# Attention and expert kernel on one core: the two heads' scores as 64-row products on the halves of the array

## The chip, the cores and the metric

The kernel runs on one core of one Trainium2 chip. The metric is the device time in microseconds (us) of that core from launch to end; lower is better. The engines are named as in the profile: PE (TensorE matmuls), PEld (its weight loads), DVE (VectorE), ACT (ScalarE), POOL (GpSimd), SP (SyncE, which issues all DMAs here). Matmuls write to banks of PSUM; the kernel's tiles of 128 x 512 fp32 take one bank each, and it uses eight.

## The reference

Attention over 8 batches, 8 heads, 576 positions, head size 64, then one feed-forward block over the 4608 tokens. Heads 0 to 3 see a local window, heads 4 to 7 a strided set:

```python
scores = scale * np.matmul(q, k.transpose(0, 1, 3, 2))
rel = pos[:, None] - pos[None, :]
mask_local = (rel >= 0) & (rel < 32)
mask_strided = (rel >= 0) & (pos[None, :] % 32 == pos[:, None] % 32)
scores = np.where(masks, scores, -1e9)          # local for h < 4, else strided
attn = exp(scores - max) / (sum + 1e-9)
x = (attn @ v), heads side by side              # 4608 x 512
h = x @ w_in                                    # 512 -> 2048
out = (h * erf(softplus(h))) @ w_out            # 2048 -> 512
```

## The kernel before, in words

Attention is cut into 96 pieces: 8 batches, four pairs of heads (`hp`; 0 and 1 local, 2 and 3 strided), three parts `j` of the sequence. A piece has up to two blocks of `n` queries against 128 keys: `n` is 96 for a local piece; for a strided one, where positions are regrouped by their residue modulo 32, it is 126 with two blocks for `j` 0 and 1, and 72 with one block for `j` 2. The two heads of a pair lie on partitions 0 to 63 and 64 to 127.

`scores` (L261) makes one fp32 product per block over all 128 partitions: the stationary operand is the keys of both heads, the moving operand has the queries of head 0 with zeros on partitions 64 to 127, beside the queries of head 1 with zeros on 0 to 63. So both heads' scores come out side by side in one bank `s`. Then, in this order, `mask` (DVE, L282, adds the mask while it copies to `sm`), `maxi` (POOL, L287, the maximum over partitions), `sub` (DVE, L296), `exp` (ACT, L300), `av` (PE, L304, into bank `pav`), `total`, `invert` and `norm` (DVE, L315 to L329), `transp` (PE, L335, into bank `pt`), `split_hi` (ACT, L353) and `split_lo_x` (DVE, L358), which write the tokens to a ring as a high and a low half (`xhi`, `xlo`).

Batches 0 and 1 differ: with `pe_mask` the mask is added on PE by a bf16 product with the identity (L271), and ACT copies the result (L279). In batch 0 (`early`) the maximum is subtracted on PE too (L291), inside the bank, which `exp` then reads; there `s` comes from the tag `h` (three banks) and `pav` from an `o` bank. In all other batches `s` and `pav` share the tag `ps` (two banks) with `pt`, which takes it in every batch.

The feed-forward block works in 12 chunks of 384 tokens, each in 16 tiles of 128 hidden units. A tile has 12 products `mm1` (L457, three terms of a high and low split) into a bank of tag `h`, a chain of ACT (L465, L495) and DVE (L462, L492, L498) steps, and 9 products `mm2` (L527) into three banks `o`. The weights arrive as 64-bit words and are unpacked by DVE (L408, L415, L421, L429) and ACT (L426). In the first part of the run PE fills idle time with products that nobody reads (`warm`, L638).

The order on every engine is written out by a planner (`Plan.order`). Each step has an engine, an estimated duration, a due time (`key`), predecessors, tiles that it takes and tiles that it uses. The planner goes through simulated time and always emits, for each engine, the ready step with the earliest due time; a step that takes a tile is ready only once the users of the tile that held that buffer before are done. Due times of pieces and expert tiles come from constants at the top (`PRO`, `SLOT`, `A0K` and others). At run time semaphores enforce the same dependencies in the emitted order.

Of the kernel before, what the change touches and what calls it, by code (L numbers as in the profile page):

```python
# [18 lines left out]
P = 128  # L19
# [21 lines left out]
RB = 7  # L41
NA = S // 32
QS = RB * NA
WL = 2 * 2 * QL + 2 * QL + 32
WS = 2 * 2 * QS + 2 * P
WV = 2 * 2 * (D + 1)
NCON = 2 * QL + QS + P
NEG = -1.0e30
# [40 lines left out]
class Plan:  # L89
# [18 lines left out]
    def _ready(self, op, live):  # L108
        t = op.earliest
        for p in op.after:  # L110
            if p.end is None:
                return None
            t = max(t, p.end + (self.SAME if p.eng == op.eng else self.LATENCY)[op.eng])
        for b in op.new:
            order = live.setdefault(b.tag, [])
            n = len(order) - self.bufs[b.tag]
            if n >= 0:
                for u in order[n].users:
                    if u.end is None:
                        return None  # L120
                    t = max(t, u.end + (self.SAME if u.eng == op.eng else self.LATENCY)[op.eng])
        return t
# [46 lines left out]
def attention_moe(  # L169
# [37 lines left out]
    def buf(pool, tag, shape, name, dtype=F32):  # L207
        def make():
            return pools[pool].tile(shape, dtype, tag=tag, name=name, bufs=bufs[tag])

        return Buf(tag, make)
# [8 lines left out]
    def piece(b, hp, j, key, dt, ring, pe_mask=False, pool_sub=False, early=False):  # L220
# [8 lines left out]
        pid = f"{b}_{hp}_{j}"  # L229
        qk = buf("apool", "qk", [P, WS], f"qk_{pid}")  # L230
        v = buf("apool", "v", [P, 2, 2, D + 1], f"v_{pid}")
        s = buf("ps_h", "h", [P, 512], f"s_{pid}") if early else buf("ps_a", "ps", [P, 512], f"s_{pid}")
        sm = buf("apool", "sm", [P, 4 * QS], f"sm_{pid}")
        mx = buf("apool", "mx", [P, 4 * QS], f"mx_{pid}")
        pav = buf("ps_o", f"o{hp % 2}", [P, 512], f"av_{pid}") if early else buf("ps_a", "ps", [P, 512], f"av_{pid}")
# [4 lines left out]
        def load_qk():  # L240
            if loc:
                yield nc.sync.dma_start(qk[:, :WL], qk_loc[b, hp, j])
            else:
                w = nblk * (2 * n + P)
                yield nc.sync.dma_start(qk[:, :w], qk_str[b, hp - 2, j, :, :w])

        def load_v():
            w = nblk * 2 * (D + 1)
            yield nc.sync.dma_start(v.tile.rearrange("p b h d -> p (b h d)")[:, :w], v_all[b, hp, j, :, :w])

        def masks():
            if loc:
                m = mask_l if j == 0 else mask_l[:, 1:2]
                return m.broadcast_to([P, 2, 2, n]), "p (b h q) -> p b h q", dict(b=2, h=2)
            return mask_s[:, :, :n].broadcast_to([P, units, n]), "p (u q) -> p u q", dict(u=units)

        def scores():
            k0, step = units * n, n if loc else P
            for blk in range(nblk):
                dst = s[:, blk * 2 * n : (blk + 1) * 2 * n]  # L260
                yield nc.tensor.matmul(  # L261
                    dst,
                    qk[:, k0 + blk * step : k0 + blk * step + P],
                    qk[:, blk * 2 * n : (blk + 1) * 2 * n],
                    start=blk == 0,
                    stop=not pe_mask,
                    skip_group_check=True,
                )
                if pe_mask:
                    m = (mask_l[:, int(j > 0 or blk > 0)] if loc else mask_s[:, :, :n]).broadcast_to([P, 2, n])  # L270
                    yield nc.tensor.matmul(  # L271
                        dst.rearrange("p (h q) -> p h q", h=2), ident_b, m, start=False, stop=True,
                        skip_group_check=True,
                    )

        def mask():
            src, dst = s[:, :cols], sm[:, :cols]
            if pe_mask:
                yield nc.scalar.copy(dst, src)  # L279
            else:  # L280
                m, r, sizes = masks()
                yield nc.vector.tensor_tensor(  # L282
                    out=dst.rearrange(r, **sizes), in0=src.rearrange(r, **sizes), in1=m, op=ALU.add
                )

        def maxi():
            yield nc.gpsimd.partition_all_reduce(mx[:, :cols], sm[:, :cols], P, ReduceOp.max)  # L287

        def sub():
            if early:  # L290
                yield nc.tensor.matmul(  # L291
                    s[:, :cols], neg, mx[:, :cols], start=False, stop=True, skip_group_check=True
                )
            else:
                d = sm[:, :cols]
                yield (nc.gpsimd if pool_sub else nc.vector).tensor_tensor(out=d, in0=d, in1=mx[:, :cols], op=ALU.subtract)  # L296

        def exp():
            d = sm[:, :cols]
            yield nc.scalar.activation(d, s[:, :cols] if early else d, AF.Exp, scale=1.0 / D**0.5)  # L300

        def av():
            for u in range(units):
                yield nc.tensor.matmul(  # L304
                    pav[:n, u * (D + 1) : (u + 1) * (D + 1)],
                    sm[:, u * n : (u + 1) * n],
                    v[:, u // 2, u % 2, :],
                    start=True,
                    stop=True,
                )  # L310
# [48 lines left out]

        add = plan.add  # L360
        w = nblk * n
        lq = add("sp", P * 4 * (WL if loc else nblk * (2 * n + P)) / 3.6e5, key - 8.0, load_qk, new=[qk])
        lv = add("sp", P * 4 * nblk * 2 * (D + 1) / 3.6e5, key - 7.9, load_v, new=[v])
        per = max(2 * n / 600.0, 0.213) + (2 * n / 2400.0 if pe_mask else 0.0)
        o_s = add("pe", 0.02 + nblk * per, key, scores, [lq, *o_con], [s, sm], [qk])
        if pe_mask:
            o_m = add("act", act(cols, 0.06), key + 0.1, mask, [o_s], [], [s, sm])
        else:
            o_m = add("dve", dve(cols), key + 0.1, mask, [o_s], [], [s, sm])
        o_x = add("pool", 0.4 + cols * 0.0028, key + 0.2, maxi, [o_m], [mx], [sm], earliest=6.7)  # L370
        if early:
            o_b = add("pe", cols / 600.0, key + dt, sub, [o_x], [], [mx, s])
        elif pool_sub:
            o_b = add("pool", 0.1 + cols / 450.0, key + 0.3, sub, [o_x], [], [mx, sm])
        else:
            o_b = add("dve", dve(cols), key + dt, sub, [o_x], [], [mx, sm])
        o_e = add("act", act(cols), key + dt + 0.1, exp, [o_b], [], [sm, s] if early else [sm])
        o_v = add("pe", 0.00174*n * units, key + dt + 0.2, av, [o_e, lv], [pav, xn], [sm, v])
        o_r = add("dve", 0.07, key + 1.5 * dt, total, [o_v], [rc], [pav])
        o_r = add("dve", 0.1, key + 1.5 * dt, invert, [o_r], [], [rc])  # L380
# [269 lines left out]
def _layout(q, k, v):  # L650
    import numpy as np

    f32 = np.float32
    hl = H // 2

    def pairs_t(a):

        a = a.reshape(B, 2, 2, S, D).transpose(0, 1, 2, 4, 3)
        return np.ascontiguousarray(a).reshape(B, 2, 2 * D, S)

    def resid(a):
        return np.ascontiguousarray(a.reshape(B, hl, NA, 32, D).transpose(0, 1, 3, 2, 4)).reshape(B, hl, S, D)

    qk_loc = np.zeros((B, 2, 3, P, WL), f32)
    qk_str = np.zeros((B, 2, 3, P, WS), f32)
    v_all = np.zeros((B, 4, 3, P, 2, 2, D + 1), f32)
    v_all[..., D] = 1.0

    ql, kl = pairs_t(q[:, :hl]), pairs_t(k[:, :hl])
    kl = np.concatenate([np.zeros((B, 2, 2 * D, 32), f32), kl], axis=3)  # L670
    vl = v[:, :hl].reshape(B, 2, 2, S, D)
    vl = np.concatenate([np.zeros((B, 2, 2, 32, D), f32), vl], axis=3)
    qb = qk_loc[..., : 4 * QL].reshape(B, 2, 3, P, 2, 2, QL)
    for j in range(3):
        for blk in range(2):
            i = 2 * j + blk
            for h in range(2):
                qb[:, :, j, h * D : (h + 1) * D, blk, h] = ql[:, :, h * D : (h + 1) * D, i * QL : (i + 1) * QL]
                v_all[:, :2, j, :, blk, h, :D] = vl[:, :, h, i * QL : i * QL + P]
        qk_loc[:, :, j, :, 4 * QL :] = kl[..., j * 2 * QL : j * 2 * QL + 2 * QL + 32]  # L680
    qk_loc[..., : 4 * QL] = qb.reshape(B, 2, 3, P, 4 * QL)

    qs, ks, vs = resid(q[:, hl:]), resid(k[:, hl:]), resid(v[:, hl:])
    qs, ks = pairs_t(qs), pairs_t(ks)
    vs = vs.reshape(B, 2, 2, S, D)
    for j in range(3):
        nblk = 2 if j < 2 else 1
        n = QS if j < 2 else S - 4 * QS
        for blk in range(nblk):
            p0 = (2 * j + blk) * QS  # L690
            for h in range(2):
                hs, c0 = slice(h * D, (h + 1) * D), (2 * blk + h) * n
                qk_str[:, :, j, hs, c0 : c0 + n] = qs[:, :, hs, p0 : p0 + n]
            k0 = nblk * 2 * n + blk * P
            qk_str[:, :, j, :, k0 : k0 + n] = ks[..., p0 : p0 + n]
            for h in range(2):
                v_all[:, 2:, j, :n, blk, h, :D] = vs[:, :, h, p0 : p0 + n]
    return qk_loc, qk_str, v_all.reshape(B, 4, 3, P, WV)
# [45 lines left out]
```

## Time and profile before

| | us |
|---|---|
| median of 3 runs | 994.0 |
| lowest and highest | 993.76, 994.02 |
| the profiled execution, own time | 993.13 |
| its span (first to last instruction) | 991.2 |
| PE busy | 979.5 |
| DVE busy | 728.7 |
| ACT busy | 654.7 |
| POOL busy | 152.8 |

How to read the rows: a row of grouped instructions has line, engine, operation, written tile <- read tiles, shape and count, then busy us and mean ns of one, then the engine's idle time just before them with what ended it. In a row of the timeline or of the chain the first two numbers are the start and the length in us, and `x4` says that four neighbours were merged. Matmuls are pipelined, so the lengths of neighbours overlap; the time that a group really takes on PE is read from start to start.

### The profile page before, as it was taken

To read this page: it belongs to the slowest core of one execution; us is meant where nothing else is said; L and a number is where in the kernel's file an instruction comes from. 1 tells how busy PE (TensorE), PEld (TensorE's weight loads), DVE (VectorE), ACT (ScalarE), POOL (GpSimd) and SP (SyncE) were. 2 spreads that over 40 slices of the span, in tenths; PEclk is the share of its full clock that TensorE was granted. 3 is DMA by queue.
4 is the path that set the end of the run, shared out by engine and by line. 5 is a ranking of instruction groups with operands and counts; after the bars stand their busy time and mean duration, and the time that the engine had idled before them with its cause. 6 is when DMAs were issued, how large, how long until landed. Compare 5 with 4: busy or idle time off the path is not lost.

```text
span 991.2 us, 15250 instructions
## 1 busy us (share of the span) xinstructions
PE 979.5 (99%) x5443; PEld 885.6 (89%) x5443; DVE 728.7 (74%) x1619; ACT 654.7 (66%) x1481; POOL 152.8 (15%) x100
## 2 busy tenths in 40 slices
PE   8999999999999999999999999999999999999998
PEld 6788999999899989999899999999899999999997
DVE  6999997677677776676777776776767776665664
ACT  4676777567566666666765665766766576766765
POOL 3534111111112110011112110111111210000000
PEclk9999999999999999999999999999999999999999
DMA  9994211111222211111222220211112220000000
GB/s 310 308 338 144 63 35 59 40 40 53 71 62 82 62 37 38 46 53 27 80 58 73 71 63 19 70 40 40 49 53 66 63 63 1 32 2 0 32 1 33
DMA packets 37659, 68.76 MB, mean 69 GB/s; under 512 B 4176, under 2 KB 18640, under 8 KB 37584
## 3 DMA queue, kind: packets, MB, share of 16 engines
q1 hardware_dynamic: 37584, 67.80, 22.1%
q8 instruction: 43, 0.70, 0.3%
q14 instruction: 32, 0.26, 0.1%
HBM read 58.34 MB, written 9.44 MB: 68 GB/s over the span
## 4 chain that ended last, share of the span: by engine, by line
PE 91%; DVE 8%; ACT 0%; issue 0%; DMA 0%
PE h L457 39%; PE o L527 39%; PE s L261 5%; PE av L304 5%; DVE w L415 1%; PE t L335 1%; DVE w L421 1%; DVE pair L429 1%; DVE a L462 1%; DVE w L408 1%; DVE glo L498 1%; DVE b L492 0%; DVE xlo L358 0%; DVE b L462 0%; PE warm L638 0%
## 5 line engine op out<-in xcount | busy, mean ns | idle before, releaser
L527 PE MATMUL o<-pair,ghi 128*128 128x512 f32 x1152 | 372.3, 404 | 0.0
L457 PE MATMUL h<-xhi,pair 128*128 128x384 f32 x1536 | 306.7, 341 | 1.4 <-DVE b L492 1.4
L457 PEld LDWEIGHTS h<-xhi,pair 128*128 128x128 f32 x1536 | 271.9, 188 | 15.7 <-DVE b L492 3.8
L465 ACT ACTIVATE b<-b 128x384 f32<-128x384 f32 x384 | 199.7, 521 | 104.2 <-DVE b L462 101.6
L287 POOL PARTITION_ALL_REDUCE mx<-sm x96 | 152.6, 1594 | 664.1 <-DVE sm L282 568.7
L527 PEld LDWEIGHTS o<-pair,ghi 128*128 128x128 f32 x1152 | 207.0, 188 | 28.0
L527 PE MATMUL o<-pair,glo 128*128 128x512 f32 x576 | 225.9, 392 | 0.0
L457 PE MATMUL h<-xlo,pair 128*128 128x384 f32 x768 | 165.9, 337 | 0.0
L498 DVE TENSOR_TENSOR glo<-b,ghi 128x384 fp32r<-128x384 f32 x192 | 110.5, 576 | 60.3 <-ACT ghi L495 59.8
L462 DVE SCALAR_TENSOR_TENSOR a<-h,a 128x384 f32<-128x384 f32 x192 | 106.4, 554 | 64.9 <-ACT a L465 63.3
L457 PEld LDWEIGHTS h<-xlo,pair 128*128 128x128 f32 x768 | 137.2, 187 | 0.0
L462 DVE SCALAR_TENSOR_TENSOR a<-a,h 128x384 f32<-128x384 f32 x192 | 105.5, 549 | 40.7 <-ACT b L465 38.6
L465 ACT ACTIVATE b<-a 128x384 f32<-128x384 f32 x192 | 100.5, 524 | 47.6 <-DVE glo L498 47.1
L527 PEld LDWEIGHTS o<-pair,glo 128*128 128x128 f32 x576 | 108.1, 188 | 24.1
L495 ACT CAST ghi<-b 128x384 fp32r<-128x384 f32 x192 | 97.9, 510 | 46.8 <-PE o L527 41.6
L492 DVE TENSOR_TENSOR b<-b,h 128x384 f32<-128x384 f32 x192 | 105.1, 547 | 31.2 <-ACT b L465 30.9
L465 ACT ACTIVATE a<-a 128x384 f32<-128x384 f32 x192 | 100.2, 522 | 26.6 <-DVE a L462 24.3
L465 ACT ACTIVATE a<-h 128x384 f32<-128x384 f32 x192 | 92.7, 483 | 33.4 <-PE h L457 32.3
L462 DVE SCALAR_TENSOR_TENSOR b<-b,a 128x384 f32<-128x384 f32 x192 | 110.5, 576 | 3.2
L304 PEld LDWEIGHTS av<-v,sm 128*96 128x96 f32 (+2 forms) x704 | 78.0, 171 | 7.8 <-ACT sm L300 1.5
L261 PE MATMUL s<-qk 128*128 128x192 f32 (+2 forms) x352 | 83.4, 351 | 0.1
L304 PE MATMUL av<-v,sm 128*96 128x65 f32 (+2 forms) x704 | 77.9, 251 | 1.1 <-ACT sm L279 0.7
(34 smaller groups left out, 588.4 us busy)
## 6 DMA issues: line engine op xcount, KB each, us to landing
qk<-qk_loc SPq DMA_DIRECT2D x48, 304.0 KB, 2.8
qk<-qk_str SPq DMA_DIRECT2D x32, 380.0 KB, 3.2
v<-v_all SPq DMA_DIRECT2D x80, 130.0 KB, 2.1
out<-ob SPq DMA_DIRECT2D x36, 256.0 KB, 2.1
words<-w_in SPq DMA_DIRECT2D x16, 512.0 KB, 5.6
words<-w_out SPq DMA_DIRECT2D x16, 512.0 KB, 5.9
qk<-qk_str SPq DMA_DIRECT2D x16, 136.0 KB, 2.1
v<-v_all SPq DMA_DIRECT2D x16, 65.0 KB, 1.9
```

The source lines that it names most:

```text
L261: yield nc.tensor.matmul(dst, qk[:, k0 + blk * step : k0 + blk * step + P], qk[:, blk * 2 * n : (blk + 1) * 2 * n], start=blk == 0, stop=n ...
L287: yield nc.gpsimd.partition_all_reduce(mx[:, :cols], sm[:, :cols], P, ReduceOp.max)
L304: yield nc.tensor.matmul(pav[:n, u * (D + 1) : (u + 1) * (D + 1)], sm[:, u * n : (u + 1) * n], v[:, u // 2, u % 2, :], start=True, stop=True,)
L335: yield nc.tensor.transpose(pt[:, blk * n : (blk + 1) * n], xn[:n, 2 * blk : 2 * blk + 2, :].rearrange("p h d -> p (h d)"), ident[:n, :n],)
L408: yield nc.vector.tensor_scalar(out=w.tile.bitcast(U32), in0=words[:, :, 1], scalar1=0x07FFFFFF, scalar2=3, op0=ALU.bitwise_and, op1=ALU.l ...
L457: yield nc.tensor.matmul(ph[:, :CH], win[4 * s + cc][:, w, fs], x[cc][:, c0 : c0 + CH], start=(i == 0), stop=(i == len(terms) - 1))
L462: yield nc.vector.scalar_tensor_tensor(out=out, in0=in0, scalar=scalar, in1=in1, op0=op0, op1=op1)
L465: yield nc.scalar.activation(dst, src, func, bias=bias[i], scale=scale)
L492: yield nc.vector.tensor_tensor(out=bb.tile, in0=bb.tile, in1=ph[:, :CH], op=ALU.mult)
L495: yield nc.scalar.copy(ghi.tile, bb.tile)
L498: yield nc.vector.tensor_tensor(out=glo.tile, in0=bb.tile, in1=ghi.tile.bitcast(F32), op=ALU.subtract)
L527: yield nc.tensor.matmul(po.tile, g[:, ts], wout[f][:, w], start=(f == 0 and i == 0), stop=(f == NFC - 1 and i == 2),)
```

## The change

Each block's score product becomes two, one for each head, over 64 partitions (0 to 63 and 64 to 127). The queries lie without zeros in one block of columns for both heads. Each head writes a bank of its own, `s[0]` and `s[1]`, with all blocks of the head side by side; in batch 0 `s[0]` comes from the tag `h` and `s[1]` from `ps`, in the others both come from `ps`. The order of columns in `sm` changes from block-head to head-block, and `av` reads accordingly. The mask on DVE, the mask product on PE, the copy on ACT, and in batch 0 the subtracting product and the exponential, run once per head on half the columns. The loads of queries and keys get narrower. The planner counts two tiles of one tag in one step, and is given new durations.

```diff
-WL = 2 * 2 * QL + 2 * QL + 32
-WS = 2 * 2 * QS + 2 * P
+WL = 2 * QL + 2 * QL + 32
+WS = 2 * QS + 2 * P
...
-        for b in op.new:
+        for i, b in enumerate(op.new):
             order = live.setdefault(b.tag, [])
-            n = len(order) - self.bufs[b.tag]
+            n = len(order) - self.bufs[b.tag] + sum(x.tag == b.tag for x in op.new[:i])
...
-        s = buf("ps_h", "h", [P, 512], f"s_{pid}") if early else buf("ps_a", "ps", [P, 512], f"s_{pid}")
+        s = [
+            buf("ps_h", "h", [P, 512], f"s{h}_{pid}") if early and h == 0 else buf("ps_a", "ps", [P, 512], f"s{h}_{pid}")
+            for h in range(2)
+        ]
...
         def scores():
-            k0, step = units * n, n if loc else P
+            k0, step = half, n if loc else P
             for blk in range(nblk):
-                dst = s[:, blk * 2 * n : (blk + 1) * 2 * n]
-                yield nc.tensor.matmul(
-                    dst,
-                    qk[:, k0 + blk * step : k0 + blk * step + P],
-                    qk[:, blk * 2 * n : (blk + 1) * 2 * n],
-                    start=blk == 0,
-                    stop=not pe_mask,
-                    skip_group_check=True,
-                )
-                if pe_mask:
...
+                for h in range(2):
+                    rows = slice(h * D, (h + 1) * D)
                     yield nc.tensor.matmul(
+                        s[h][:, blk * n : (blk + 1) * n],
+                        qk[rows, k0 + blk * step : k0 + blk * step + P],
+                        qk[rows, blk * n : (blk + 1) * n],
+                        start=blk == 0,
+                        stop=not pe_mask,
                         skip_group_check=True,
                     )
+            if pe_mask:
+                for h in range(2):
+                    yield nc.tensor.matmul(
+                        s[h][:, :half].rearrange("p (b q) -> p b q", b=nblk), ident_b, masks(),
+                        start=False, stop=True, skip_group_check=True,
+                    )
 
         def mask():
-            src, dst = s[:, :cols], sm[:, :cols]
...
+            for h in range(2):
+                src, dst = s[h][:, :half], sm[:, h * half : (h + 1) * half]
...
         def exp():
...
+            if early:
+                for h in range(2):
+                    yield nc.scalar.activation(
+                        sm[:, h * half : (h + 1) * half], s[h][:, :half], AF.Exp, scale=1.0 / D**0.5
+                    )
...
-        per = max(2 * n / 600.0, 0.213) + (2 * n / 2400.0 if pe_mask else 0.0)
-        o_s = add("pe", 0.02 + nblk * per, key, scores, [lq, *o_con], [s, sm], [qk])
+        per = 0.235 + (2 * n / 2400.0 if pe_mask else 0.0)
+        o_s = add("pe", 0.08 + nblk * per, key, scores, [lq, *o_con], [*s, sm], [qk])
...
-            o_m = add("dve", dve(cols), key + 0.1, mask, [o_s], [], [s, sm])
+            o_m = add("dve", dve(cols) + 0.067, key + 0.1, mask, [o_s], [], [*s, sm])
```

More of the change, by code (lines that the diff above doesn't have):

```diff
@@ L243, in load_qk @@
             else:
-                w = nblk * (2 * n + P)
+                w = nblk * (n + P)
                 yield nc.sync.dma_start(qk[:, :w], qk_str[b, hp - 2, j, :, :w])
@@ L249, in load_v @@
             yield nc.sync.dma_start(v.tile.rearrange("p b h d -> p (b h d)")[:, :w], v_all[b, hp, j, :, :w])
+        half = nblk * n
         def masks():
@@ L253, in masks @@
                 m = mask_l if j == 0 else mask_l[:, 1:2]
-                return m.broadcast_to([P, 2, 2, n]), "p (b h q) -> p b h q", dict(b=2, h=2)
-            return mask_s[:, :, :n].broadcast_to([P, units, n]), "p (u q) -> p u q", dict(u=units)
+                m = m.rearrange("p b h q -> p b (h q)")
+                return m.broadcast_to([P, 2, n]) if j else m
+            return mask_s[:, :, :n].broadcast_to([P, nblk, n])
         def scores():
-            k0, step = units * n, n if loc else P
+            k0, step = half, n if loc else P
@@ L259, in scores @@
             for blk in range(nblk):
-                dst = s[:, blk * 2 * n : (blk + 1) * 2 * n]
-                yield nc.tensor.matmul(
-                    dst,
-                    qk[:, k0 + blk * step : k0 + blk * step + P],
-                    qk[:, blk * 2 * n : (blk + 1) * 2 * n],
-                    start=blk == 0,
-                    stop=not pe_mask,
-                    skip_group_check=True,
-                )
-                if pe_mask:
-                    m = (mask_l[:, int(j > 0 or blk > 0)] if loc else mask_s[:, :, :n]).broadcast_to([P, 2, n])
-                    yield nc.tensor.matmul(
-                        dst.rearrange("p (h q) -> p h q", h=2), ident_b, m, start=False, stop=True,
+                for h in range(2):
+                    rows = slice(h * D, (h + 1) * D)
+                    yield nc.tensor.matmul(
+                        s[h][:, blk * n : (blk + 1) * n],
[3 more added lines that the diff above has]
+                        stop=not pe_mask,
@@ L273, in scores @@
                         skip_group_check=True,
                     )
-        def mask():
-            src, dst = s[:, :cols], sm[:, :cols]
[L278 to L284, printed above, removed]
+            if pe_mask:
[4 more added lines that the diff above has]
+                    )
@@ L286, in maxi @@
+        def mask():
+            for h in range(2):
+                src, dst = s[h][:, :half], sm[:, h * half : (h + 1) * half]
+                if pe_mask:
+                    yield nc.scalar.copy(dst, src)
+                else:
+                    yield nc.vector.tensor_tensor(
+                        out=dst.rearrange("p (b q) -> p b q", b=nblk),
+                        in0=src.rearrange("p (b q) -> p b q", b=nblk), in1=masks(), op=ALU.add,
+                    )
         def maxi():
@@ L290, in sub @@
             if early:
-                yield nc.tensor.matmul(
-                    s[:, :cols], neg, mx[:, :cols], start=False, stop=True, skip_group_check=True
-                )
+                for h in range(2):
+                    yield nc.tensor.matmul(
+                        s[h][:, :half], neg, mx[:, h * half : (h + 1) * half], start=False, stop=True,
+                        skip_group_check=True,
+                    )
             else:
@@ L298, in exp @@
         def exp():
-            d = sm[:, :cols]
-            yield nc.scalar.activation(d, s[:, :cols] if early else d, AF.Exp, scale=1.0 / D**0.5)
+            if early:
+                for h in range(2):
+                    yield nc.scalar.activation(
+                        sm[:, h * half : (h + 1) * half], s[h][:, :half], AF.Exp, scale=1.0 / D**0.5
+                    )
+            else:
+                yield nc.scalar.activation(sm[:, :cols], sm[:, :cols], AF.Exp, scale=1.0 / D**0.5)
         def av():
@@ L305, in av @@
                     pav[:n, u * (D + 1) : (u + 1) * (D + 1)],
-                    sm[:, u * n : (u + 1) * n],
+                    sm[:, (u % 2) * half + u // 2 * n : (u % 2) * half + (u // 2 + 1) * n],
                     v[:, u // 2, u % 2, :],
@@ L361, in piece @@
         w = nblk * n
-        lq = add("sp", P * 4 * (WL if loc else nblk * (2 * n + P)) / 3.6e5, key - 8.0, load_qk, new=[qk])
+        lq = add("sp", P * 4 * (WL if loc else nblk * (n + P)) / 3.6e5, key - 8.0, load_qk, new=[qk])
         lv = add("sp", P * 4 * nblk * 2 * (D + 1) / 3.6e5, key - 7.9, load_v, new=[v])
-        per = max(2 * n / 600.0, 0.213) + (2 * n / 2400.0 if pe_mask else 0.0)
-        o_s = add("pe", 0.02 + nblk * per, key, scores, [lq, *o_con], [s, sm], [qk])
+        per = 0.235 + (2 * n / 2400.0 if pe_mask else 0.0)
+        o_s = add("pe", 0.08 + nblk * per, key, scores, [lq, *o_con], [*s, sm], [qk])
         if pe_mask:
-            o_m = add("act", act(cols, 0.06), key + 0.1, mask, [o_s], [], [s, sm])
+            o_m = add("act", act(cols, 0.15), key + 0.1, mask, [o_s], [], [*s, sm])
         else:
-            o_m = add("dve", dve(cols), key + 0.1, mask, [o_s], [], [s, sm])
+            o_m = add("dve", dve(cols) + 0.067, key + 0.1, mask, [o_s], [], [*s, sm])
         o_x = add("pool", 0.4 + cols * 0.0028, key + 0.2, maxi, [o_m], [mx], [sm], earliest=6.7)
         if early:
-            o_b = add("pe", cols / 600.0, key + dt, sub, [o_x], [], [mx, s])
+            o_b = add("pe", cols / 600.0, key + dt, sub, [o_x], [], [mx, *s])
         elif pool_sub:
@@ L376, in piece @@
             o_b = add("dve", dve(cols), key + dt, sub, [o_x], [], [mx, sm])
-        o_e = add("act", act(cols), key + dt + 0.1, exp, [o_b], [], [sm, s] if early else [sm])
+        o_e = add("act", act(cols, 0.18 if early else 0.093), key + dt + 0.1, exp, [o_b], [], [sm, *s] if early else [sm])
         o_v = add("pe", 0.00174*n * units, key + dt + 0.2, av, [o_e, lv], [pav, xn], [sm, v])
@@ L672, in _layout @@
     vl = np.concatenate([np.zeros((B, 2, 2, 32, D), f32), vl], axis=3)
-    qb = qk_loc[..., : 4 * QL].reshape(B, 2, 3, P, 2, 2, QL)
     for j in range(3):
@@ L677, in _layout @@
             for h in range(2):
-                qb[:, :, j, h * D : (h + 1) * D, blk, h] = ql[:, :, h * D : (h + 1) * D, i * QL : (i + 1) * QL]
                 v_all[:, :2, j, :, blk, h, :D] = vl[:, :, h, i * QL : i * QL + P]
-        qk_loc[:, :, j, :, 4 * QL :] = kl[..., j * 2 * QL : j * 2 * QL + 2 * QL + 32]
-    qk_loc[..., : 4 * QL] = qb.reshape(B, 2, 3, P, 4 * QL)
+        qk_loc[:, :, j, :, : 2 * QL] = ql[..., j * 2 * QL : (j + 1) * 2 * QL]
+        qk_loc[:, :, j, :, 2 * QL :] = kl[..., j * 2 * QL : j * 2 * QL + 2 * QL + 32]
     qs, ks, vs = resid(q[:, hl:]), resid(k[:, hl:]), resid(v[:, hl:])
@@ L690, in _layout @@
             p0 = (2 * j + blk) * QS
[L691 to L694, printed above, removed]
+            qk_str[:, :, j, :, blk * n : (blk + 1) * n] = qs[..., p0 : p0 + n]
+            k0 = nblk * n + blk * P
             qk_str[:, :, j, :, k0 : k0 + n] = ks[..., p0 : p0 + n]
```

## The prediction

> **What bounds the kernel now.** I read the page first for the engine shares and for the chain of work that ended last, then the clock row (9 in all 40 slices, so no throttle enters the argument), then the chain in order of time to see where its engine changes.
>
> ```profile
> span 991.2 us, 15250 instructions
> ...
> PE 979.5 (99%) x5443; PEld 885.6 (89%) x5443; DVE 728.7 (74%) x1619; ACT 654.7 (66%) x1481; POOL 152.8 (15%) x100
> ...
> PE 91%; DVE 8%; ACT 0%; issue 0%; DMA 0%
> PE h L457 39%; PE o L527 39%; PE s L261 5%; PE av L304 5%; DVE w L415 1%; PE t L335 1%; DVE w L421 1%; DVE pair L429 1%; DVE a L462 1%; DVE w L408 1%; DVE glo L498 1%; DVE b L492 0%; DVE xlo L358 0%; DVE b L462 0%; PE warm L638 0%
> ...
> L527 PE MATMUL o<-pair,ghi 128*128 128x512 f32 x1152 | 372.3, 404 | 0.0
> ...
> L261 PE MATMUL s<-qk 128*128 128x192 f32 (+2 forms) x352 | 83.4, 351 | 0.1
> ```
>
> The tensor engine (PE) is the bound, and the line the change rewrites, L261, carries 5% of the chain, about 50 us. The 83.4 us of the last row are sums of overlapping durations, so I do not price from them. The chain ordered by time shows that the first part has another bound:
>
> ```profile
> 15.06 0.60 DVE w L415
> ...
> 77.97 0.61 DVE w L421
> ...
> 78.61 0.62 ACT pair L426
> ...
> 80.17 0.89 PE av L304 x8
> ```
>
> Between these first two rows the chain is almost wholly VectorE (DVE) unpacking expert weights; from 80 us it is PE to the end. Stretches of the span, busy us of PE, PE's weight loads, DVE, ACT, POOL, then clock, DMA share and rate:
>
> ```profile
> 0.00:78.60 78.60, 72.22 (x473) 58.54 (x474) 70.64 (x158) 49.85 (x135) 33.45 (x21) 1.00 0.93 321
> 78.60:991.20 912.60, 907.25 (x4973) 827.09 (x4971) 658.06 (x1462) 604.87 (x1346) 119.37 (x79) 1.00 0.16 48
> ```
>
> So PE time saved after 78.6 us is worth its full amount. PE time saved before it is worth nothing, as idle PE there is filled with warm-up products (L638), and only the moment at which the first expert product can start counts. DVE after 78.6 us is busy 72%: DVE work added there is covered by PE's queue.
>
> **The score products, the term that decides.** One fp32 product shows in the trace as two weight loads and two matmuls, so a two-block piece is four of each.
>
> ```profile
> 303.09 0.38 PE L335 MATMUL t<-ident,xn 126*128 126x126 f32 x2
> ...
> 303.31 0.82 PE L261 MATMUL s<-qk 128*128 128x192 f32 x4
> ...
> 303.82 0.77 PE L527 MATMUL o<-pair,ghi 128*128 128x512 f32 x2
> ...
> 304.66 0.62 PE L527 MATMUL o<-pair,ghi 128*128 128x512 f32 x2
> ...
> 305.30 0.41 DVE L358 TENSOR_TENSOR xlo<-t,xhi 128x252 fp32r<-128x252 f32 x1
> 305.35 1.57 PE L457 MATMUL h<-xhi,pair 128*128 128x384 f32 x8
> ...
> 308.15 0.99 PE L304 MATMUL av<-v,sm 128*126 128x65 f32 x8
> ...
> 308.98 0.33 PE L335 MATMUL t<-ident,xn 96*128 96x96 f32 x2
> ...
> 313.37 1.01 PE L261 MATMUL s<-qk 128*128 128x252 f32 x4
> ...
> 314.03 1.74 PE L457 MATMUL h<-xhi,pair 128*128 128x384 f32 x8
> ```
>
> A local piece (96 queries) starts at 303.31. The product behind it is recorded from 303.82, but as 0.77 instead of 0.62, so it really begins 0.15 later: 303.97 - 303.31 = 0.66 us. A strided piece (126): 314.03 + (1.74 - 1.57) - 313.37 = 0.83 us. Four matmuls of 192 and 252 columns give 0.165 and 0.21 each, about 0.00085 us per streamed column; the one-block piece (72) by that rate: 2 x 144 x 0.00085 = 0.24 us.
>
> The price of a weight load comes from the attention-value products: eight with 65 streamed columns (0.055 us each by the rate) start 0.83 us before what follows, 0.104 us each for 126 stationary columns. They are paced by their loads: 0.00083 us per column, so 0.106 us for 128.
>
> After the change a two-block piece has 8 loads of 128 columns and 8 matmuls of 96 or 126 columns (0.08 or 0.107 each), four of each on either half of the array. The trace holds no half-array product. The lower bound is that the halves run wholly beside each other: each half's chain is 4 loads, 0.42 us (one block: 0.21). The upper bound is that loads pass one at a time, 8 x 0.106 = 0.85 us (0.42). I take the halves as overlapping, since they share neither partitions nor banks, plus one load that has no cover because products issue in order (both passes of one head come before the other's, so the second half starts one load late), plus a little for changing kind, for which these are the nearest rows:
>
> ```profile
> 81.65 0.48 PE L261 MATMUL s<-qk 128*128 128x192 f32 x2
> ...
> 82.05 0.52 PE L261 MATMUL s<-qk 128*128 128x192 f32 x2
> ```
>
> The second pair, right behind a bf16 mask product, is 0.04 longer. So 0.42 + 0.106 + 0.03 = 0.55 us for either two-block piece, and 0.21 + 0.106 = 0.32 for the one-block piece. The number of pieces on the PE-bound part is that of the DVE masks (batches 2 to 7; batches 0 and 1 are masked on PE and I credit them nothing, their bound being 0 to 1.5 us for the few after 78.6):
>
> ```profile
> L282 DVE TENSOR_TENSOR sm<-s,con 128x384 f32<-128x384 f32 x36 | 19.9, 554 | 8.1 <-PE s L261 8.1
> ...
> L358 DVE TENSOR_TENSOR xlo<-t,xhi 128x192 fp32r<-128x192 f32 x48 | 16.8, 349 | 2.9 <-ACT xhi L353 2.9
> ...
> L282 DVE TENSOR_TENSOR sm<-s,con 128x504 f32<-128x504 f32 x24 | 16.3, 680 | 3.5 <-PE s L261 3.2
> ...
> L282 DVE TENSOR_TENSOR sm<-s,con 128x144 f32<-128x144 f32 x12 | 3.6, 303 | 1.4 <-PE s L261 1.4
> ```
>
> 36 x (0.66 - 0.55) + 24 x (0.83 - 0.55) - 12 x (0.32 - 0.24) = 4.0 + 6.7 - 1.0 = 9.7 us gained. Lower bound of cost: 36 x 0.24 + 24 x 0.41 + 12 x 0.03 = 18.8 us gained. Upper: 36 x 0.19 + 24 x 0.02 + 12 x 0.18 = 9.5 us lost.
>
> The Trainium skill, "TensorE: Matmul & The Clock Gate", Part 3, says that products on different row groups run at once, a pack lasting one product plus about 4 ns for each further tile, and that a weight load overlaps running products only where the row group differs. The second half does not hold here: the 0.104 us step above is a load's time, not load plus product, on one full array. By the first half loads would cost nothing; that is a rival below.
>
> **The DVE masks.** One mask of 384 columns (0.554) becomes two of 192; a DVE pass of that size that also reads a bank takes 0.349 (L358), so +0.14 us on each of 72 pieces, 10 us on DVE. Cover: PE's backlog; without it, a piece's maximum on POOL starts 0.14 us later. I cost it at nothing.
>
> **Masks on PE, copies and exponentials of batches 0 and 1.**
>
> ```profile
> L279 ACT COPY sm<-s 128x384 f32<-128x384 f32 x12 | 5.8, 480 | 6.7 <-PE s L271 5.9 <-PE t L335 0.8
> ...
> L353 ACT CAST xhi<-t 128x192 fp32r<-128x192 f32 x48 | 15.1, 314 | 11.4 <-PE t L335 11.4
> ...
> L300 ACT ACTIVATE sm<-s 128x384 f32<-128x384 f32 x6 | 3.0, 492 | 3.9 <-PE s L291 3.7
> ```
>
> Two half copies instead of one: 2 x 0.314 - 0.480 = 0.15 us more ACT for 24 pieces, and as much for the 12 early exponentials: 5.4 us, of an ACT busy 49.85 of 78.6 us, behind the DVE chain. Mask and subtract products keep their columns.
>
> **Loads.**
>
> ```profile
> qk<-qk_loc SPq DMA_DIRECT2D x48, 304.0 KB, 2.8
> ```
>
> A local load drops from 608 to 416 columns, to 208 KB, a strided one from 760 to 508. No DMA is added, so nothing queues longer on SP. The weights that share the early 321 GB/s come sooner, but DVE, already busy 70.64 of 78.6 us, is what consumes them: no gain taken, up to 2 us possible.
>
> **Banks, the cost side.** Each piece now holds two score banks. In batches 2 to 7 both come from the tag `ps`, which has two, shared with `av` and `t`: scores need both empty at once. The rows at 303 show what that forbids: the transpose at 303.09 held one until its last reader ended at 305.71, and the scores started at 303.31. They must now come 2.4 us later; PE has L527 and L457 work in between if the planner's order has it there. I take 0 and keep 2.4 us per misplaced wait. In batch 0 the second bank is from `ps` too, held until the exponential:
>
> ```profile
> 13.14 0.54 PE L261 MATMUL s<-qk 128*128 128x192 f32 x2
> ...
> 14.70 0.54 PE L261 MATMUL s<-qk 128*128 128x192 f32 x2
> ...
> 15.60 0.33 PE L335 MATMUL t<-ident,xn 96*128 96x96 f32 x2
> ...
> 18.00 0.91 PE L291 MATMUL s<-mx,neg 128*128 128x384 f32 x2
> ...
> 50.80 1.85 PE L457 MATMUL h<-xhi,pair 128*128 128x384 f32 x8
> ```
>
> Pieces 3 and 4, begun at 13.14 and 14.70, would hold both banks until the exponential behind 18.00: 18.00 + 0.91 + 0.49 = 19.4. The transpose at 15.60 needs one and would wait 3.8 us. If that lag lasts through ten pieces, the first expert product moves from 50.80 to 54.6, and PE, busy from there on, has lost 3.8 us; DVE can unpack weights meanwhile and give part back. Between 0 and 3.8 I take 2.
>
> **The sum.** 991.2 - 9.7 + 2 = 983.5 us of span. The profiled execution's own time is 993.13, 1.9 outside the span: 985.4. The median of the runs, 994.0, lies 0.9 above that execution: 986.
>
> **The rivals.** A measurement of this kernel tells about 0.2%, 2 us, from no change.
>
> (a) Loads pass one at a time. For: the trace shows only one load stream, pacing `av` at 0.104 us. Against: the halves read different partitions. Place: L261's successor at 0.85 us a piece. It decides from 0.66 us on a local and 0.83 on a strided piece. Time 994 + 9.5 + 2 = 1005.
>
> (b) Changing between whole and half array empties the array. Two changes a piece; the gain is gone when each costs 0.053 us above my sum (7.7 us over 144 changes); a bare load in front of each, 0.106, would make it 994 - 7.7 + 15.3 = 1002. For: nothing in the trace covers such a change. Against: the 0.04 us of the mask rows. Likely time 994. The Trainium skill, "TensorEngine Tiling (Array Packing)", Key Properties, says just this: changing the tiling mode, not merely the tile, drains the engine. No run here shows it yet.
>
> (c) PE stands before scores for a bank. Four waits of the 2.4 us kind eat the gain, eight bring 994 - 7.7 + 19 = 1005. Against: PE idles 0.1 us before L261 in the whole run, so the planner's times hold.
>
> (d) Loads are free, the halves paced by streaming: four product times a piece, 0.32 and 0.43, one block 0.12: 36 x 0.34 + 24 x 0.40 + 12 x 0.12 = 23.3 gained, 994 - 23.3 + 2 = 973. Against: the `av` step. This is what the page's pack rule would make of it.
>
> **How the numbers follow.** The forecast has 0.60, (a) 0.17, (b) 0.10, (c) 0.08, (d) 0.05. Faster: forecast and (d), 0.65; same: most of (b), 0.08; slower: (a), (c) and the rest of (b), 0.27. The likeliest case alone spans 975 (18.8 gained, no lag) to 990 (3.8 lag and one bank wait). The range for 8 in 10 leaves out (d) and the far ends of (b) and (c): 975 to 1006, the upper end being (a).
>
> **What will show it.** Score rows with 64 rows and 96, 126 or 72 columns, twice as many; from the first one's start to the real begin of what follows, 0.55 us for either two-block piece (0.85 under (a), 0.66 or more under (b)). Idle PE before scores released by DVE would be (c). The first `h` product later than 50.80 shows the batch-0 lag. What would make me wrong is above all the load price on halves, which no row of before contains.

## The result, and the profile after

The changed kernel takes 1027.4 us (median of 4 runs, 1022.1 to 1028.7) against 994.0 before: ratio 1.0327, 95% interval 1.029 to 1.0363. 986 was forecast, in a range of 975 to 1006. The profiled execution, the fastest of the four, took 1022.08 with a span of 1020.3; of the 29 us between its span and that of before, the traces place most at the very start.

The page of the changed kernel, shares and the first two slice rows:

```profile
span 1020.3 us, 16370 instructions
...
PE 1004.7 (98%) x5941; PEld 886.9 (87%) x5941; DVE 730.8 (72%) x1691; ACT 658.2 (65%) x1517; POOL 155.5 (15%) x100
...
PE   8799999999999999999999999999999999999998
...
PEclk9899999999999999999999999999999999999999
```

PE is still the bound for most of the run and has 25 us more of busy time. Warm-up products are a good part of it: 229 instead of 111, busy for 31.0 us instead of 16.1, as this row of grouped instructions shows, and they stand only ahead of the first expert product.

```profile
L654 PE MATMUL warm<-con 128*128 128x256 bf16 x229 | 31.0, 289 | 3.8 <-DVE con L574 3.8
```

The timeline of PE has that first product (`h`, now L473) at 69.52 us; it was at 50.80.

```profile
69.52 1.30 PE L473 MATMUL h<-xhi,pair 128*128 128x384 f32 x6
```

So 18.7 us are lost before the PE-bound part begins. The second chunk of 384 tokens begins 24 us later than before, and the last 29.

Now the score pieces (timeline of PE). The first three rows are a local piece with its neighbours, the next three a strided one:

```profile
301.08 0.40 PE L543 MATMUL o<-pair,glo 128*128 128x512 f32 x1
301.41 0.69 PE L269 MATMUL s<-qk 64*128 64x96 f32 x8
302.03 1.68 PE L473 MATMUL h<-xhi,pair 128*128 128x384 f32 x8
...
307.68 0.39 PE L543 MATMUL o<-pair,glo 128*128 128x512 f32 x1
308.00 0.71 PE L269 MATMUL s<-qk 64*128 64x126 f32 x8
308.64 0.74 PE L543 MATMUL o<-pair,ghi 128*128 128x512 f32 x2
```

One `o` product takes 0.23 from start to start, so the one at 301.08 is through at 301.31. The scores start only at 301.41. The `h` products behind are recorded from 302.03 and last 1.68 instead of 1.57, so they really begin at 302.14. The piece takes 302.14 - 301.31 = 0.83 us (0.66 before), the strided one 308.76 - 307.91 = 0.85 (0.83 before). Over all pieces of batches 2 to 7 the medians are 0.82, 0.84 and, for one block, 0.57 (0.65, 0.85 and 0.24 before, read the same way). Yet the halves do work beside each other: eight loads of 128 columns would need 0.85 one after the other, and here eight start within the 0.52 us of this row, less the length of the last:

```profile
301.41 0.52 PEld L269 LDWEIGHTS s<-qk 64*128 64x128 f32 x8 [0.36 <-DVE b L508]
```

What costs is the way in and out: 0.10 us pass before the first load, and that load stands uncovered. At the end a further pair of half-array products would have started at 301.93, one step of 0.11 behind the last pair; the next whole-array load starts 0.10 later, at 302.03, and stands uncovered too.

### The profile page after: what moved, and what is told of

The parts are those of the page before. It is cut to its first block, busy times and chain, and to the rows that moved or that the text cites. A ratio compares the mean times of both kernels' runs of the same rounds, so it can differ in the third digit from the quotient of the medians.

```text
span 1020.3 us, 16370 instructions
## 1 busy us (share of the span) xinstructions
PE 1004.7 (98%) x5941; PEld 886.9 (87%) x5941; DVE 730.8 (72%) x1691; ACT 658.2 (65%) x1517; POOL 155.5 (15%) x100
## 4 chain that ended last, share of the span: by engine, by line
PE 91%; DVE 7%; POOL 1%; ACT 1%; DMA 0%; issue 0%; SPq 0%; POOLq 0%; ACTq 0%
PE o L543 40%; PE h L473 38%; PE av L320 5%; PE s L269 5%; PE t L351 1%; DVE w L431 1%; DVE w L437 1%; DVE pair L445 1%; POOL mx L296 1%; DVE w L424 1%; DVE a L478 1%; PE warm L654 1%; PE s L301 0%; DMA qk<-qk_loc 0%; DVE glo L514 0%; DVE b L508 0%
## 5 line engine op out<-in xcount | busy, mean ns | idle before, releaser
L473 PE MATMUL h<-xhi,pair 128*128 128x384 f32 x1536 | 304.8, 340 | 0.4 <-DVE b L508 0.4
L473 PEld LDWEIGHTS h<-xhi,pair 128*128 128x128 f32 x1536 | 271.0, 188 | 14.0 <-DVE b L508 1.4
L296 POOL PARTITION_ALL_REDUCE mx<-sm x96 | 155.3, 1621 | 693.8 <-DVE sm L290 592.8
L543 PEld LDWEIGHTS o<-pair,ghi 128*128 128x128 f32 x1152 | 202.1, 188 | 33.4
L473 PE MATMUL h<-xlo,pair 128*128 128x384 f32 x768 | 165.8, 338 | 0.0
L473 PEld LDWEIGHTS h<-xlo,pair 128*128 128x128 f32 x768 | 137.3, 188 | 0.0
L478 DVE SCALAR_TENSOR_TENSOR b<-b,a 128x384 f32<-128x384 f32 x192 | 107.6, 561 | 3.0
L269 PEld LDWEIGHTS s<-qk 64*128 64x128 f32 x704 | 48.6, 189 | 29.1 <-issue 11.9
```

What stands on the lines that cost most here:

```text
L269: yield nc.tensor.matmul(s[h][:, blk * n : (blk + 1) * n], qk[rows, k0 + blk * step : k0 + blk * step + P], qk[rows, blk * n : (blk + 1) * n],
L473: yield nc.tensor.matmul(ph[:, :CH], win[4 * s + cc][:, w, fs], x[cc][:, c0 : c0 + CH], start=(i == 0), stop=(i == len(terms) - 1))
L478: yield nc.vector.scalar_tensor_tensor(out=out, in0=in0, scalar=scalar, in1=in1, op0=op0, op1=op1)
L543: yield nc.tensor.matmul(po.tile, g[:, ts], wout[f][:, w], start=(f == 0 and i == 0), stop=(f == NFC - 1 and i == 2),)
```

## The experiments

Theory A: in batch 0 the second score bank holds up the pieces and delays the first expert product; later only the changes between whole and half array cost. The diffs show only the lines that matter, some of them in short form, and what stands behind `#` is for the reader. Each kernel was compared with the kernel before on the same chip, whose median there was 994.3 to 994.9.

**Batch by batch.** The first two put pieces back to one 128-row product per block and one bank; the third does the change in batch 0 alone.

```diff
+HALVES = {1, 2, 3, 4, 5, 6, 7}          # e1_batch0_whole
+HALVES = {2, 3, 4, 5, 6, 7}             # e2_batches01_whole
+HALVES = {0}                            # e3_batch0_halves
...
+        halves = b in HALVES
```

> Batch 0 as before the change (one 128-row product per block, one bank of tag h), batches 1 to 7 as after it. Theory A (in batch 0 the second score bank, taken from ps and held until the exponential, holds up the pieces and delays the first expert product; later only the changes between whole and half array cost): 1002 us, 999 to 1006, first h product at 51 to 54 us instead of 69.5. Rival B (the half-array products themselves are dear, wherever they stand): 84 of 96 pieces keep them, so 1020 or more. Rival C (banks short in batches 1 to 7 cost most): 1015 or more.

Measured (e1): 1005.5 us, ratio 1.0118 (1.0097 to 1.014), first `h` at 51.67.

> Batches 0 and 1 as before the change, 2 to 7 as after it. Theory A: 1000 us, 998 to 1003; score groups of local pieces take 0.82 us from the end of the product before to the begin of the next instead of 0.66, strided ones 0.85 instead of 0.83, one-block ones about 0.5 instead of 0.24. Rival B: 1015 or more. Rival C: 1010 or more, with idle PE before scores.

Measured (e2): 1001.7, ratio 1.0071 (1.0056 to 1.0086).

> Only batch 0 as after the change, 1 to 7 as before it. Theory A: 1013 to 1020 us, first h product at about 69 us. Rival B: 12 pieces with 0.2 to 0.4 us more each, 994 to 999. Rival C: 994 to 1000.

Measured (e3): 1016.8, ratio 1.023 (1.0204 to 1.0256), first `h` at 73.6, later than the 69 expected. Batch 0 with its 12 of 96 pieces costs 22 us, batch 1 about 4 (e1 against e2), batches 2 to 7 about 7; the sum, 33, is the whole loss. Rivals B and C fall as explanations of the bulk. The waits of PE's weight loads in the changed kernel show how the late batches lose: small gaps before scores, many of them put down to no particular release:

```profile
PEld s L269 <- issue: 11.9, 45, 0.4
```

45 waits of about a quarter of a us, none over 0.4: a regular price, not a queue for a bank.

**The bank without the product.** Whole-array products, but in batch 0 each block has a bank of its own.

```diff
-            dst = s[:, blk * 2 * n : (blk + 1) * 2 * n]
+            dst = s[blk][:, : 2 * n]        # s[0] from h, s[1] from ps; batch 0
```

> Whole-array products everywhere; only in batch 0 each two-block piece puts its two blocks into two banks, h and ps, as the change does with its heads, with copies, subtractions and exponentials on half the columns. No half-array product is in it. Theory A (the bank, not the product, delays the start): as e3 within 5 us, 1008 to 1020, first h product past 60 us. Rival B: 994 to 996.

Measured (e4): 1015.9, ratio 1.0218 (1.02 to 1.0236), first `h` at 76.5. No half-array product is in this kernel, and its loss is that of e3. So the second bank, with the copies, subtractions and exponentials in two halves that come with it, causes the late start, and the half-array product does not. A run below (e11) tells the bank from the halved steps.

**Inside the late start.** The changed kernel has one maximum on POOL (L296) that lasts 8.19 us; the four of its size in batch 0 before took 1.76 to 2.77. These are rows of its timeline, of POOL, PE and DVE:

```profile
27.85 8.19 POOL L296 PARTITION_ALL_REDUCE mx<-sm  x1 [7.63 <-ACT sm L288]
...
32.80 1.27 DVE L437 SCALAR_TENSOR_TENSOR w<-words,w 128x512 uint32<-128x512 uint32 x2
34.00 0.41 DVE L424 TENSOR_SCALAR w<-words 128x512 uint32<-128x512 uint32 x1
...
36.09 2.05 PE L301 MATMUL s<-mx,neg 128*128 128x252 f32 x4 [5.41 <-POOL mx L296]
...
42.22 0.36 DVE L374 TENSOR_TENSOR xlo<-t,xhi 128x192 fp32r<-128x192 f32 x1 [7.81 <-ACT xhi L369]
```

DVE unpacks weights almost without a pause until 34.41, and POOL ends at 36.04, one ordinary maximum later. PE stands at the subtraction (L301) for 5.41 us; the transposes that the plan has behind it wait too, and DVE, whose next step in order is the last one of such a piece, idles 7.81 us. Two runs took this apart:

```diff
+            add("dve", 0.1, key - 20.0, pause, [o_x], [rp], [mx])   # e7: batch 0, copies mx[:, :1]
-        pt = buf("ps_a", "ps", [P, 512], f"t_{pid}")
+        pt = buf("ps_o", f"o{hp % 2}", ...) if early else buf("ps_a", "ps", ...)   # e11
```

> The changed kernel, and in batch 0 DVE copies one column of each maximum right where the plan has POOL's step end, so DVE stops there until POOL is through. Theory A1 (the 8.19 us maximum of piece 5 is POOL shut out while DVE unpacks weights without a pause): no maximum of batch 0 over 3.5 us, first h product 61 to 66 instead of 69.5 us, 1016 to 1024 us. Rival D (POOL itself is slow at its first call with 504 columns, whatever DVE does): the maximum still takes about 8 us, 1026 to 1030.

Measured (e7): 1013.6, ratio 1.0194 (1.018 to 1.0208), first `h` at 66.2; the long maximum falls from 8.19 to 4.61 us, not to 3.5, and the total by more than was expected. The profiled executions are 8.3 us apart, and only 3.3 of that is at the first `h`; where the rest comes from is open.

```profile
26.65 4.61 POOL L296 PARTITION_ALL_REDUCE mx<-sm  x1 [5.30 <-ACT sm L288]
...
28.95 0.68 DVE L453 TENSOR_TENSOR pair<-w,pair 128x512 fp32r<-128x512 f32 x1
31.29 0.15 DVE L392 COPY rp<-mx 128x1 f32<-128x1 f32 x1 [1.66 <-POOL mx L296]
```

DVE stops here at 29.63, and POOL ends at 31.26, 1.63 us later. In the changed kernel DVE stopped at 34.41, and POOL ended 1.63 us later too. In both kernels the maximum ends about one ordinary maximum after DVE stops, and in e7 it lasts over 3.5 us because DVE still has unpacking steps ahead of the pause. Rival D falls; the first maximum with 504 columns before, at 21.55, had taken 1.76 us. The Trainium skill, "SBUF — State Buffer", section "SBUF: two separate sides", says that a DVE instruction with two SBUF inputs and a GpSimd instruction that reads SBUF exclude each other on one pair of ports, the later one blocked for the other's whole duration. L431, L437 and L445 have two such inputs, and 8.19 against 4.61 us agrees. That POOL loses to a whole row of DVE instructions, one behind the other, is what the trace adds.

> The changed kernel, but in batch 0 the transpose writes to the o bank of its piece's av instead of a ps bank, so that the two ps banks serve scores alone. Theory A2 (the start is late because transposes stand behind two held score banks, and the next scores behind transposes): first h product at 55 to 62 us, 1010 to 1018 us. Rival E (two instead of three pieces' scores in flight is what costs): first h within 3 us of 69.5, 1024 or more.

Measured (e11): 1009.9, ratio 1.0156 (1.014 to 1.0171), first `h` at 55.8.

```profile
55.84 1.48 PE L473 MATMUL h<-xhi,pair 128*128 128x384 f32 x7
```

Taking only the transposes of batch 0 out of the tag `ps` wins back 13.7 of the 18.7 us at the start, with half-array products and halved steps left in. So most of the delay is transposes standing behind held score banks, as the prediction described it for 15.60 us. The long maximum is part of these 13.7: in e11 it takes 4.80 us without any pause on DVE. What fewer pieces in flight (rival E) and the halved steps cost besides is at most the 5.0 us that are left at the start. These 5, the 4 of batch 1 and the 7 of batches 2 to 7 add up to about the 15.6 us that e11 still loses.

**The price of going into the half array.** Batches 2 to 7 by halves as in e2, each product issued twice.

```diff
-            yield from products()
+            for _ in range(2):
+                yield from products()
```

> As e2 (batches 0 and 1 whole, 2 to 7 by halves), but every half-array product of a piece is issued twice in a row, with the same result. Theory A (a fixed price of about 0.37 us for going into and out of the half array, and 0.112 us per pair of products within): the extra products cost 0.45 us for each of 60 two-block pieces and 0.22 for each of 12 one-block ones, 30 us, so 1031 us, and the group of a two-block piece takes 0.82 + 0.45 = 1.27 us. Rival B (loads pass one at a time, 0.82 us a piece without any fixed price): 60 x 0.82 + 12 x 0.5 = 55 us more, 1057 us.

Measured (e6): 1031.2, ratio 1.0368 (1.035 to 1.0386), 29.4 us over e2. Timeline of PE, a local piece with 16 products:

```profile
301.58 0.86 PE L517 MATMUL h<-xlo,pair 128*128 128x384 f32 x4
302.37 1.14 PE L314 MATMUL s<-qk 64*128 64x96 f32 x16
303.43 0.73 PE L587 MATMUL o<-pair,ghi 128*128 128x512 f32 x2
```

Four `h` products of 0.176 end at 302.28; the `o` products, recorded with 0.73 instead of 0.62, begin at 303.54: 1.26 us. The second set costs 1.26 - 0.82 = 0.44, so a set is worth 0.44 and the way in and out 0.82 - 0.44 = 0.38, or 0.19 on average for each change. The medians over all pieces of batches 2 to 7 give 0.38 for local pieces, 0.40 for strided ones and 0.36 for one-block ones. The Trainium skill, "TensorEngine Tiling (Array Packing)", Key Properties, names this: a change of tiling mode drains the engine. It gives no figure; here the two changes cost 0.38 us, loads without cover included.

**One stay for two pieces, and the control.** Only the strided two-block pieces of batches 2 to 7 by halves; in e8 those of both strided pairs share the two banks, 252 columns each, and one stay of 16 products; in e9 each goes by itself. For the joint stay e8 also changes the order of pieces in the odd batches from 2 on, so that the two strided pieces stand side by side.

```diff
-        s[h][:, blk * n : (blk + 1) * n]
+        s[h][:, at + blk * n : at + (blk + 1) * n]   # at = 252 for the second pair, same banks
...
-            yield from products()
+            yield from products()
+            yield from mate["products"]()
```

> Only the strided two-block pieces of batches 2 to 7 by halves, and those of the two strided pairs in one stay of 16 products: both pairs' scores of a head in one bank, side by side. Everything else as before the change. Theory A: one fixed price of 0.37 us for two pieces: 0.37 + 8 x 0.112 = 1.26 us instead of 2 x 0.85 = 1.70, 12 times, 5 us gained: 989 us, 986 to 992. Rival B: 12 x (1.66 - 1.70), no gain, 993 to 995.

Measured (e8): 988.9, ratio 0.9941 (0.9925 to 0.9956).

```profile
297.76 0.87 PE L542 MATMUL h<-xlo,pair 128*128 128x384 f32 x4
298.56 1.16 PE L326 MATMUL s<-qk 64*128 64x126 f32 x16
299.65 0.73 PE L612 MATMUL o<-pair,ghi 128*128 128x512 f32 x2
```

By the same reading 299.76 - 298.46 = 1.30 us for two pieces that took 1.70. This version beats both kernels, the one before by 0.6%.

> As e8, but each strided two-block piece of batches 2 to 7 makes its 8 half-array products by itself, with two changes of the array for each piece. Theory A: 24 x (0.84 - 0.85), nothing gained or lost on PE: 993 to 996; the difference to e8 is the fixed price of 12 stays, 4.4 us, plus 0.5. Rival B: the same as e8.

Measured (e9): 993.6, ratio 0.999 (0.998 to 1.0): no change that can be told. The 4.6 us between e9 and e8 are what 12 stays of 0.38 come to. But e8 also has another order of pieces and takes the banks for the strided scores half as often, so it is argued, not shown, that the stays alone make this difference. Their price on PE is read from the rows.

**Banks in the late batches.**

```diff
-            dst = s[:, blk * 2 * n : (blk + 1) * 2 * n]
+            dst = s[blk][:, : 2 * n]        # both from ps; batches 2 to 7
```

> Whole-array products everywhere; in batches 2 to 7 each two-block piece puts its two blocks into two ps banks, and the DVE mask runs once per bank on half the columns, as the change does with its heads. No half-array product. Theory A (in these batches only the changes between whole and half array cost): 993 to 996. Rival C (banks short, PE stands before scores): 998 or more.

Measured (e5): 991.8, ratio 0.9968 (0.9958 to 0.9977). Two banks and two half masks cost nothing there, they gain 3 us, which no theory had. On PE the score groups keep their 0.65 and 0.85, so the gain lies elsewhere; where is open.

> e8 (strided pairs of batches 2 to 7 by halves in one stay of 16 products) with the local pieces of these batches put into two banks by blocks, as in e5. If the gains of e8 and of e5 add up: 994.9 - 5.9 - 2 = 987, 984 to 988.5. If the gain of e5 was only another order of the strided pieces: 988 to 990.

Measured (e10): 989.4, ratio 0.995 (0.9937 to 0.9962). The gains of e8 and e5 do not add up. The time lies in the range that was given for another order of the strided pieces, which is a hint and no proof.

## Why the prediction was wrong, point by point

**The step that failed most** is the bank in batch 0: "Between 0 and 3.8 I take 2". The mechanism was named rightly, down to the transpose that stands behind two held banks. The size was not: e3 puts it at 22 us. I had priced the first wait and let it pass through ten pieces once. In fact the lag grows with every pair of pieces, since their scores wait for the transposes of the pair before, and those for the exponential. In the timeline of PE of the changed kernel, the transpose that stood at 15.60 comes after both subtractions:

```profile
20.83 0.82 PE L301 MATMUL s<-mx,neg 128*128 128x192 f32 x4
21.48 0.33 PE L351 MATMUL t<-ident,xn 96*128 96x96 f32 x2
...
43.64 0.71 PE L269 MATMUL s<-qk 64*128 64x126 f32 x8
```

The scores of pieces 5, 7, 9 and 11 start at 23.49, 43.64, 54.40 and 61.83, which is 4.4, 15.1, 18.9 and 19.9 us later than before. The largest step, 10.7 us, is the round with the maximum of 8.19 us, which the prediction did not have. DVE, which I let give part back, did the reverse: in the plan's order its next steps hung on the late transposes, so it idled, and when it ran without a pause POOL came late. Windows of before (first row) and after (second) between 30 and 40 us, in the order PE, weight loads, DVE, ACT, POOL:

```profile
30.00:40.00 10.00, 8.96 (x60) 6.50 (x59) 9.97 (x20) 6.62 (x20) 4.73 (x3) 1.00 0.86 276
```

```profile
30.00:40.00 10.00, 4.59 (x20) 3.30 (x18) 4.41 (x9) 0.76 (x2) 7.78 (x2) 0.74 0.65 236
```

DVE did 4.41 us of work where it had done 9.97. The chain before 78.6 us ran on DVE, so this was time lost for good.

**The score term** was wrong in its last summands. That the halves overlap held (0.44 for a set, 0.42 forecast for its chain of loads). One load without cover and the price of changing kind were taken as 0.106 + 0.03, the latter from a bf16 mask beside an fp32 product; e6 gives 0.38 for both. The reason for the 0.106, that the second half starts one load late, does not hold either: the two products of a pair start within 0.01 us of each other. (For the one-block piece the sum left the 0.03 out.) With the measured groups the sum is 36 x 0.17 + 24 x 0 + 12 x 0.33 = 10.1 us lost instead of 9.7 gained. e2 shows 7.1; that the 3 us of e5 are the difference is argued, not shown. This is rival (b), which had a chance of 0.10. A two-block piece takes 0.27 us (local) or 0.29 (strided) above the forecast 0.55, some 0.14 a change, where (b) allowed for 0.053 and at most 0.106.

**Rival (a)**, loads one at a time, gave 0.85 us a piece, close to the 0.82 and 0.84 measured, yet it is false: 16 products would have taken twice as much, and took 1.26. **Rival (c)** is excluded for batches 2 to 7 by e5. **Rival (d)** is excluded by the local pieces: a set takes 0.44 us, and streaming alone would take 0.32. **The DVE masks** cost nothing that shows; **the narrower loads** brought nothing that shows.

**Open:** what costs the 4 us of batch 1, which also has two `ps` banks a piece (in e1 PE stands 2.34 us, up to 63.20, for a step of DVE, which is busy without a pause from 60 to 64 us; e2 has no such wait, but what put DVE behind is not shown); where the 3 us of e5 come from; and why the four runs of the changed kernel range over 6.6 us.

## What to carry to other kernels

Price a half-array product with the way in and out of the half array, here 0.36 to 0.40 us a stay, and put enough products into one stay. Before a tile takes a second buffer of a shared tag, follow that tag through the busiest stage for every round, not for the first wait: a hold that crosses engines can grow from round to round. And an engine that has work to spare gives nothing back if its order is fixed and the next step is the late one.

## What the runs showed of the hardware

The wait of 5.41 us on PE, from 30.68 to 36.09, went along with a slower clock: the granted clock was 0.74 on average between 30 and 40 us, 1.00 in the window from 34.0 to 34.8 and 0.50 from 35.0 to 41.6, and the subtracting products in that time ran at about half speed. In all traces here the clock falls, other than at the end of a run, only during or within 1.4 us after waits of PE of 1.53 to 6.72 us; yet e3 has waits of 3.11 and 3.35 us at full clock, so the length of a wait does not decide alone. In the timeline of the changed kernel, four such products soon after the wait and 10 us later:

```profile
39.64 1.89 PE L301 MATMUL s<-mx,neg 128*128 128x252 f32 x4
...
49.52 1.02 PE L301 MATMUL s<-mx,neg 128*128 128x252 f32 x4
```

The warm-up products do not help here, since they stand behind the waiting product in PE's order. And the two half-array products of a pair start together: the piece of 16 in e6, at 302.37, has eight pairs in 1.06 us up to the next product, 0.11 us a pair with 0.19 for the way out taken off, which is about one load's time (0.106).
